# Combined output weights made in other slots, state sums ordered from GpSimd, one partial product in another PSUM bank

## The chip, the cores and the metric

One Trainium2 chip, one core. The metric is the device time of one execution in microseconds, as the median of several runs. The kernel before took 835.33 us (three runs, 834.94 to 835.89). Lines such as L1167 are lines of the kernel before.

## What is computed

Retention attention (scores with a decaying causal mask, no softmax) over 8 batches x 8 heads x 576 positions x 64, then a feed-forward layer with softplus on the 4608 tokens:

```python
scores = (q @ k.T) / 8                                   # per batch and head
Dmat   = where(i >= j, gamma[h] ** (i - j), 0)           # gamma[h] = 1 - 2**(-5-h)
x      = ((scores * Dmat) @ v), heads side by side       # 4608 x 512
h      = x @ w_in                                        # 512 x 2048
g      = maximum(h, 0) + log1p(exp(-abs(h)))
out    = g @ w_out                                       # 2048 x 512
```

All of it is in float32; the large products are made of three products of rounded high and low parts (`TERMS`).

## The kernel before

Tokens go in 9 units of 512. Unit 0 is worked plainly while the weights are split into high and low parts. Units 1 and 2 are worked together, and so are 3 and 4, 5 and 6, 7 and 8: two units make a 2x2 block product that needs seven instead of eight block products (Strassen's form), with sums of input blocks (`T1`, `T2`, `T3`, `NT4`) made beforehand and sums of weight blocks kept in DRAM (`sums_dram` for w_in, `outs_dram`, "outcombined" in the profile, for w_out). Units 1 and 2 use this only for the first product and for the last two of the eight weight pairs J; the last three pairs of units (s = 1, 2, 3) use it for both products.

The parts of the program in order of time:

- about 122 to 195 us: `plain_slot`, twelve slots of unit 1, slot p = 0 to 11
- about 196 to 230 us: `strassen_pair`, J = 6 and J = 7, seven products each
- about 230 to 324 us: twelve plain slots of unit 2, then the outputs of what was kept
- about 324 to 449 us: `full_pair` of s = 1, J = 0 to 7, then `full_phase`, the second product; after that s = 2 (from 506 us) and s = 3.

`product(bank, x)` is six matmuls of 512 columns into one PSUM bank, and the load of a weight block to come. The banks around the change are `acc`, the two halves of `two`, and `later["third"]`. In `full_pair` TensorE does, in this order, the products B11 (into `acc`), B21 (into `y`), T2 (`acc`), T1 (into `z`), T3 (`acc`), B22 (`z`), `second(banks[1])`, NT4 (`acc`), then the attention group (`chunk_products`), then `second(banks[0])`. After B11 ScalarE copies `acc` out (L1167, to a tile of `G[J]`), after T2 again (L1175), after T1 it copies `z` (L1179), after NT4 it copies `acc` (L1208). VectorE adds the others (L1169, L1183, L1197). A product that starts a bank anew must wait until the bank was read.

Every pair with a `group` also carries one attention group of two steps: scores, masked scores times values, the state times queries, and new state sums. `chunk_products` issues them in four stages that put two row groups of the array to work at a time. The state sums of both row groups go into one bank, `third`: the first row group's (t = 0) in stage 1, the second's (t = 1) in stage 4. A tiny copy out of the bank between them (L340, tile `mark`) makes the second wait for the first. After the group VectorE reads the scores (L242), the values (L420) and, after two softplus steps, the state sums (L270, L271, L280).

`full_pair` returns three closures that the next pair runs: `head` after B21, `differences` after T2, and `last_difference` after its `c12` sum (L1246, L1247, then the `jobs` of that pair). ScalarE's logarithms of `c22` (L464, L468, L469) and its copy L1208 come behind these jobs in program order. The program order is the order on each engine (`tc.manual_schedule()`).

The combined output weights are made from `wouts` by `whole_out` (L638, two sums of 512 columns on VectorE), `combine_out` (L648 to L651, four of 256 columns; the last one, L651, still reads the tile that the first cast overwrites), `split_out` (two ScalarE casts L655, two VectorE differences L659) and a store of two 512 KB transfers (L667). There are eight of them, j = 0 to 7. `whole_in(j, at)` puts the sums into the place of the weights 2at and 2at+1; from s = 1 on, `G[at]` is placed there too, so L1167 of pair J = at waits until such a store has read it. Before the change j = 0 and 1 are made in the two `strassen_pair`s, 2, 3 and 4 in slots 4 to 11 of unit 2 (place 0, 1, 2), 5, 6 and 7 among the jobs of `full_pair` at s = 1 (places 4 and 5, and a spare pair of `quad` buffers).

`queue_store` puts the two transfers in the list `queued`; one or more of it is issued at each product, and the rest behind NT4, all on SyncE's queue.

Of the kernel before, what the change touches and what calls it, by code (L numbers as in the profile page):

```python
# [55 lines left out]
RING = 7  # L56
QUADS = 6
B11, B22, B21, T1, T3, T2, NT4 = range(7)
# [25 lines left out]
def retention_softplus_ffn(ctx: ExitStack, tc, first, whole, others, consts, w, out):  # L84
# [50 lines left out]
    place_weights(wpool, WOUT1)  # L135

    live = {}
    states = {}
# [80 lines left out]
    def sums_mm(m, s, t, h):  # L219

        L = live[m]
        start, follows = _chunk_kind(m // 2)
        if follows if t else start != HC:
            nc.tensor.matmul(L["T"][rows[h], t, part[s]], L["kp"][rows[t], s, rows[h]], L["v"][rows[t], s, rows[h]],  # L224
                             start=True, stop=True, skip_group_check=True)

# [83 lines left out]

    def chunk_products(steps, done, marker=nc.vector.tensor_copy):


# [13 lines left out]
        def together(*products):  # L327
            for j in range(2):
                for s in range(2):
                    for o in range(2):  # L330
                        for g, (f, which) in enumerate(products):
                            if j < len(which):
                                t, h = (o, g) if f is scores_mm else (g, o)
                                clear = (j == s == 0,) if f is values_mm else ()
                                f(which[j], s, t, h, *clear)

        together((sums_mm, steps), (scores_mm, steps))
        if steps and _chunk_kind(steps[0] // 2)[0] != HC:
            mark = later["mark"].tile([P, 1], F32, tag="mark", name="mark")
            marker(mark, third[:, 0, 0:1])  # L340
        together((scores_mm, steps), (values_mm, done))
        together((values_mm, done), (cross_mm, done))
        together((cross_mm, done), (sums_mm, steps))


# [601 lines left out]
    def half_b22(i):  # L947
# [10 lines left out]
        (9, finish_combined, 2, nc.vector), (10, prepare_split, 4), (10, prepare_sums, 5), (10, half_b22, 3),  # L958
        (11, prepare_store, 4), (11, finish_combined, 3, nc.vector), (11, prepare_head, 5),
        *[(5 + 2 * j, raw_store, j) for j in range(4)])  # L960
    starts = schedule(*[(3 + 2 * i, start_combined, i) for i in range(CPU)])
# [9 lines left out]
    def strassen_pair(s, J, group, rest, last=False, extra=None):  # L971
# [4 lines left out]
        c = [q[:, n] for q in (quad(), quad()) for n in range(2)]  # L976
        y, z = two[:, 0] if s + 1 < NSUPER else later["third"], two[:, 1]
        product(acc, B11, True)
# [25 lines left out]
        nc.vector.tensor_add(c[2], z, c[2])  # L1004
        if extra is not None:
            combine_rest(raws["out", extra])
        ab2 = logs(c[2])
# [5 lines left out]
        softplus_rest(g, ab)  # L1013
        softplus(c[2], ab2)
        nc.sync.dma_start(kept_dram[J][:, 0], ab2)
        ab3 = logs(c[1])
# [10 lines left out]
        queued_some(len(queued))  # L1027
        if extra is not None:
            combine_store(outs_dram[extra], raws.pop(("out", extra)))
        if group:  # L1030
            chunk_products(*group)
            coming_steps = next_steps(group[0]) if s == 0 and J == NJ - 1 else []
            group_out(*group, between=(finish,))
            for k in coming_steps:
# [22 lines left out]

    extras = {(0, NJ - 2): 0, (0, NJ - 1): 1}
    for s in range(FULL):
# [16 lines left out]
        if first:  # L1076
# [6 lines left out]
                (4, whole_in, 2, 0), (6, combine_out, 2), (7, split_out, 2), (8, store_out, 2),  # L1083
                (8, whole_in, 3, 1), (8, combine_out, 3), (9, split_out, 3), (10, store_out, 3),
                (10, whole_in, 4, 2), (10, combine_out, 4), (11, split_out, 4))
            starts = schedule(*[(min(6 + 2 * i, 2 * first - 1), start_combined, i) for i in range(CPU)])
# [20 lines left out]
        for n, J in enumerate(range(first, NJ)):  # L1107
# [5 lines left out]
            while stores:  # L1113
                prepare_rest(stores[0])
                prepare_store(stores.pop(0))
            if n == 0:
                store_out(4)
            kept_parts(u2, J, kept[n], 1)
# [41 lines left out]
    def full_pair(s, J, group, rest, jobs, more):  # L1160
# [3 lines left out]
        c11, c12, c21, c22 = (g_slot(J, n) for n in range(4))  # L1164
        y, z = two[:, 0], two[:, 1]
        product(acc, B11, True)
# [21 lines left out]
        if not parts_of:  # L1188
            parts_of.extend(moe.tile([P, 2, T], F32R, tag="g", name="parts") for _ in range(2))
            parts_of.extend(later["quad"].tile([P, 2, T], F32R, tag="quad", name="parts") for _ in range(SPLITS - 2))  # L1190
            spare.extend(quad() for _ in range(QUADS - SPLITS + 2))
            banks.extend([ps_y.tile([P, T], F32, tag=f"y{2 * n + m}", name="sum") for m in range(2)] for n in range(2))
# [17 lines left out]
        if group:  # L1210
            chunk_products(*group, nc.scalar.copy)
        ab3 = logs(c12)
# [103 lines left out]
    for s in range(FULL, NSUPER):  # L1316
# [5 lines left out]
        if s == FULL:  # L1322
            for at, f, *args in ((0, whole_in, 5, 4), (0, combine_out, 5), (1, split_out, 5), (1, queue_store, 5),
                                 (2, whole_in, 6, 5), (2, combine_out, 6), (3, split_out, 6), (3, queue_store, 6),
                                 (3, lambda: whole_out(7, spare[:2])), (4, combine_out, 7), (5, split_out, 7),
                                 (5, queue_store, 7)):
                job(at, f, *args)
# [74 lines left out]
```

## Time and profile before

| | |
|---|---|
| median of 3 runs | 835.33 us |
| the profiled execution | 836.63 us, of which the span from the first to the last instruction 834.8 us |
| granted TensorE clock, mean | 0.998 |
| matmul busy | 818.0 us, 98% of the span |
| VectorE, ScalarE, GpSimd busy | 77%, 66%, 20% of the span |
| DMA | 209.93 MB, mean 251 GB/s |

TensorE does matmuls nearly all the time, so the shares of the other engines tell little; what can be read are the places where TensorE sat idle, and what ended each of them. Matmul ends are modelled, so lateness is best read from starts.

### The profile page before, as it was taken

The page shows a single profiled execution, that of the slowest core. Times are in us where ns is not written, and L with a number is a line of the kernel's source. Part 1 is how long each engine was busy: PE and PEld are TensorE (multiplying, and loading weights), DVE is VectorE, ACT ScalarE, POOL GpSimd, SP SyncE. Part 2 cuts the span into 40 slices and gives each one's busy share as a digit, 9 for nine tenths or more (in the row PEclk, how much of TensorE's full clock was granted, in tenths as well). Part 3 has the DMA queues.
Part 4 walks back from the last instruction along what each step waited for, and adds up shares of the span by engine and source line. Part 5 has one row for each costly group of instructions (what it writes and reads, how often), then busy time and mean ns, then how long its engine had stood idle before and what let it go on. Part 6 is the DMA issues. An engine that isn't in the chain of part 4 may idle for free.

```text
span 834.8 us, 19042 instructions
## 1 busy us (share of the span) xinstructions
PE 818.0 (98%) x7322; PEld 666.7 (80%) x7322; DVE 646.6 (77%) x1069; ACT 548.7 (66%) x970; POOL 165.3 (20%) x214
## 2 busy tenths in 40 slices
PE   8999999999999999999999999999999999999998
PEld 6788888887778877877777888888878888888886
DVE  5899975878777897688899995767889955555886
ACT  6778754547744545776777575677785658878653
POOL 3312322440221453112113000211110002212100
PEclk9999999999999999999999999999999999999999
DMA  9888879787789984688888777877856686666675
GB/s 362 305 293 306 303 263 347 256 282 255 243 300 347 322 316 165 216 272 268 265 269 256 215 216 234 263 240 244 254 159 210 207 257 191 194 193 193 193 215 170
DMA packets 149257, 209.93 MB, mean 251 GB/s; under 512 B 10800, under 2 KB 114736, under 8 KB 149168
## 3 DMA queue, kind: packets, MB, share of 16 engines
q1 hardware_dynamic: 149168, 208.72, 75.9%
q8 instruction: 58, 0.95, 0.5%
q14 instruction: 31, 0.25, 0.1%
HBM read 166.74 MB, written 41.94 MB: 250 GB/s over the span
## 4 chain that ended last, share of the span: by engine, by line
PE 69%; DVE 16%; ACT 7%; DMA 4%; issue 3%; POOL 0%; SPq 0%; DVEq 0%; ACTq 0%; POOLq 0%
PE sum L1144 18%; PE acc L839 15%; PE two L839 10%; PE y L491 9%; PE third L839 3%; PE two L1144 3%; PE h L457 2%; PE acc L1144 2%; PE third L1144 2%; PE third L224 2%; ACT parts L1134 1%; DVE g L1154 1%; DVE parts L1138 1%; DVE ab L476 1%; PE two L208 1%
## 5 line engine op out<-in xcount | busy, mean ns | idle before, releaser
L839 PE MATMUL acc<-xt,ring 128*128 128x512 f32 x768 | 193.6, 390 | 1.7 <-DVE quad L1012 0.9
L1144 PE MATMUL sum<-parts,ring 128*128 128x512 f32 x720 | 174.0, 392 | 0.0
L839 PEld LDWEIGHTS acc<-xt,ring 128*128 128x128 f32 x768 | 143.8, 188 | 33.2 <-DVE quad L1012 1.8
L1134 ACT CAST parts<-g 128x512 fp32r<-128x512 f32 x168 | 102.9, 621 | 88.0 <-DVE g L1154 29.9
L1144 PEld LDWEIGHTS sum<-parts,ring 128*128 128x128 f32 x720 | 133.8, 188 | 28.6 <-DVE parts L1138 0.3
L1138 DVE TENSOR_TENSOR parts<-g,parts 128x512 fp32r<-128x512 f32 x168 | 118.5, 727 | 38.0 <-ACT parts L1134 35.7
L491 PE MATMUL y<-wout,g 128*128 128x512 f32 x576 | 140.7, 393 | 0.8 <-DVE g L484 0.8
L491 PEld LDWEIGHTS y<-wout,g 128*128 128x128 f32 x576 | 106.9, 188 | 24.7 <-DVE g L484 1.6
L839 PE MATMUL two<-xt,ring 128*128 128x512 f32 x480 | 122.7, 391 | 0.9 <-DVE quad L981 0.8
L839 PEld LDWEIGHTS two<-xt,ring 128*128 128x128 f32 x480 | 89.5, 188 | 22.0 <-DVE xs L420 1.4
L469 ACT ACTIVATE ab<-ab 128x512 f32<-128x512 f32 x120 | 75.9, 632 | 3.8
L468 ACT ACTIVATE ab<-ab 128x512 f32<-128x512 f32 x120 | 75.9, 633 | 3.5
L1154 DVE SCALAR_TENSOR_TENSOR g<-g,ab 128x512 f32<-128x512 f32 x96 | 67.0, 710 | 7.5 <-ACT ab L469 7.3
L201 POOL TENSOR_TENSOR qv<-qv,consts_sb 128x256 f32<-128x256 f32 x61 | 47.6, 780 | 115.2 <-DMA qv<-others 114.3
L480 ACT CAST g<-ab 128x512 fp32r<-128x512 f32 x44 | 27.3, 621 | 48.2 <-DVE ab L476 36.0
L263 POOL COPY sx<-s 64x256 f32<-64x256 f32 (+1 forms) x34 | 14.1, 414 | 196.3 <-PE third L224 157.7
L457 PE MATMUL h<-xt,win 128*128 128x512 f32 x192 | 47.3, 395 | 1.4 <-DVE x L401 0.7
L282 POOL TENSOR_TENSOR s<-s,consts_sb 128x256 f32<-128x256 f32 (+1 forms) x31 | 20.3, 656 | 135.8 <-DVE s L280 118.3
L464 ACT ACTIVATE ab<-g 128x512 f32<-128x512 f32 x72 | 45.1, 627 | 0.0
L484 DVE TENSOR_TENSOR g<-ab,g 128x512 fp32r<-128x512 f32 x44 | 32.2, 732 | 14.8 <-ACT g L480 14.1
L1241 POOL TENSOR_TENSOR g<-g 128x512 f32<-128x512 f32 x10 | 14.1, 1408 | 149.2 <-DVE g L1154 149.2
L457 PEld LDWEIGHTS h<-xt,win 128*128 128x128 f32 x192 | 35.3, 188 | 9.5 <-DVE win L577 1.4
(190 smaller groups left out, 1356.2 us busy)
## 6 DMA issues: line engine op xcount, KB each, us to landing
ring<-split SPq DMA_DIRECT2D x126, 256.0 KB, 4.6
ring<-combined SPq DMA_DIRECT2D x104, 256.0 KB, 3.5
ring<-outcombined SPq DMA_DIRECT2D x96, 256.0 KB, 3.4
qv<-others SPq DMA_DIRECT2D x61, 320.0 KB, 5.0
ring<-outsplit SPq DMA_DIRECT2D x72, 256.0 KB, 3.6
wst<-w SPq DMA_DIRECT2D x32, 512.0 KB, 5.8
keys<-others SPq DMA_DIRECT2D x61, 256.0 KB, 5.0
split<-win SPq DMA_DIRECT2D x16, 512.0 KB, 6.8
```

The costliest lines, as they stand in the source:

```text
L201: nc.gpsimd.tensor_mul(v, v, f.unsqueeze(2).broadcast_to([P, 4, D]))
L457: nc.tensor.matmul(h, wins[p][:, a, kt * P:(kt + 1) * P], xt[:, b, T1 + kt // 2, kt % 2], start=(n == 0), stop=(n == 3 * NKT - 1))
L464: nc.scalar.activation(ab, h, AF.Abs)
L468: nc.scalar.activation(ab, ab, AF.Exp, scale=-1.0)
L469: nc.scalar.activation(ab, ab, AF.Ln, bias=1.0)
L484: nc.vector.tensor_sub(g[:, LO], ab, g[:, HI].bitcast(F32))
L491: nc.tensor.matmul(ys[u][tt], g[:, a, tt * P:(tt + 1) * P], wouts[p][:, b], start=(p == 0 and n == 0), stop=(p == NF - 1 and n == 2))
L839: nc.tensor.matmul(bank, w[:, ta, kt * P:(kt + 1) * P], xt[:, tb, x, kt], start=start and k == 0, stop=k == 5, skip_group_check=True)
L1134: nc.scalar.copy(t[:, HI], g_slot(J, n))
L1138: nc.vector.tensor_sub(t[:, LO], g_slot(J, n), t[:, HI].bitcast(F32))
L1144: nc.tensor.matmul(bank[m], w[:, a, m * P:(m + 1) * P], t[:, b], start=start and n == 0, stop=n == 2, skip_group_check=True)
L1154: nc.vector.scalar_tensor_tensor(c, c, 0.0, ab, op0=ALU.max, op1=ALU.add)
```

## The change

- `QUADS` goes from 6 to 8 buffers.
- In `full_pair` and `strassen_pair`, `z` (the products T1 and B22) goes to `third` and no longer to the second half of `two`.
- In the attention groups of `full_pair` (`marker` None) the mark is a GpSimd memset of one column, ordered by hand behind the last state sum of the first row group and ahead of the first of the second. All other groups keep the copy on ScalarE or VectorE.
- j = 0 is made in slots 0 to 3 of unit 1. j = 1 stays in `strassen_pair` J = 7, but its two L659 come behind a softplus (L476), and its store behind the attention group and the loads that follow it.
- j = 4 leaves slots 10 and 11 of unit 2 and is made in pair 0 and 1 of s = 1. The work in `last_difference` becomes: pair 0 sums and combination of 4 (place 2); pair 1 split and store of 4, sums and combination of 5 (place 3); pair 2 split and store of 5, sums of 6 (place 4); pair 3 combination, split and store of 6, sums of 7 (place 5); pair 4 combination, split and store of 7. Before it was: pair 1 sums and combination of 5; pair 2 split and store of 5; pair 3 sums and combination of 6; pair 4 split and store of 6, sums of 7; pair 5 combination of 7; pair 6 split and store of 7.

```diff
-QUADS = 6
+QUADS = 8
...
+    ordered = mybir.DependencyInfo(mybir.DependencyClass.Sync, mybir.DependencyReason.DATA)
...
     def chunk_products(steps, done, marker=nc.vector.tensor_copy):
+        halves = [], []
...
-                                f(which[j], s, t, h, *clear)
+                                product_of = f(which[j], s, t, h, *clear)
+                                if product_of is not None:
+                                    halves[t].append(product_of)
 
         together((sums_mm, steps), (scores_mm, steps))
-        if steps and _chunk_kind(steps[0] // 2)[0] != HC:
+        if halves[0] and marker is None:
+            mark = nc.gpsimd.memset(later["mark"].tile([P, 1], F32, tag="mark", name="mark"), 0.0).ins
+            tc.add_manual_dep(mark, halves[0][-1].name, ordered, reason="one bank's first row group")
+        elif steps and _chunk_kind(steps[0] // 2)[0] != HC:
             mark = later["mark"].tile([P, 1], F32, tag="mark", name="mark")
             marker(mark, third[:, 0, 0:1])
         together((scores_mm, steps), (values_mm, done))
         together((values_mm, done), (cross_mm, done))
         together((cross_mm, done), (sums_mm, steps))
+        if halves[0] and halves[1] and marker is None:
+            tc.add_manual_dep(halves[1][0], mark.name, ordered, reason="one bank's second row group")
...
+        (0, whole_out, 0), (1, combine_out, 0), (2, split_out, 0), (3, store_out, 0),
         *[(5 + 2 * j, raw_store, j) for j in range(4)])
...
     def strassen_pair(s, J, group, rest, last=False, extra=None):
-        y, z = two[:, 0] if s + 1 < NSUPER else later["third"], two[:, 1]
+        y, z = two[:, 0], later["third"]
...
         nc.vector.tensor_add(c[2], z, c[2])
-        if extra is not None:
-            combine_rest(raws["out", extra])
         ab2 = logs(c[2])
...
         softplus(c[2], ab2)
+        if extra is not None:
+            combine_rest(raws["out", extra])
...
         queued_some(len(queued))
-        if extra is not None:
-            combine_store(outs_dram[extra], raws.pop(("out", extra)))
         if group:
             chunk_products(*group)
             coming_steps = next_steps(group[0]) if s == 0 and J == NJ - 1 else []
+            if extra is not None:
+                combine_store(outs_dram[extra], raws.pop(("out", extra)))
...
-    extras = {(0, NJ - 2): 0, (0, NJ - 1): 1}
+    extras = {(0, NJ - 1): 1}
...
-                (8, whole_in, 3, 1), (8, combine_out, 3), (9, split_out, 3), (10, store_out, 3),
-                (10, whole_in, 4, 2), (10, combine_out, 4), (11, split_out, 4))
+                (8, whole_in, 3, 1), (8, combine_out, 3), (9, split_out, 3), (10, store_out, 3)                )
...
-            if n == 0:
-                store_out(4)
...
     def full_pair(s, J, group, rest, jobs, more):
-        y, z = two[:, 0], two[:, 1]
+        y, z = two[:, 0], later["third"]
...
         if group:
-            chunk_products(*group, nc.scalar.copy)
+            chunk_products(*group, None)
...
         if s == FULL:
-            for at, f, *args in ((0, whole_in, 5, 4), (0, combine_out, 5), (1, split_out, 5), (1, queue_store, 5),
-                                 (2, whole_in, 6, 5), (2, combine_out, 6), (3, split_out, 6), (3, queue_store, 6),
-                                 (3, lambda: whole_out(7, spare[:2])), (4, combine_out, 7), (5, split_out, 7),
-                                 (5, queue_store, 7)):
+            rest = [lambda: None, lambda: None, lambda: whole_in(4, 2), lambda: combine_out(4)]
+            for at, f, *args in ((0, split_out, 4), (0, queue_store, 4), (0, whole_in, 5, 3), (0, combine_out, 5),
+                                 (1, split_out, 5), (1, queue_store, 5), (1, whole_in, 6, 4), (2, combine_out, 6),
+                                 (2, split_out, 6), (2, queue_store, 6), (2, whole_in, 7, 5), (3, combine_out, 7),
+                                 (3, split_out, 7), (3, queue_store, 7)):
                 job(at, f, *args)
```

(The first number of a job is the pair that returns it; it runs in the next one. The line `spare.extend(...)` still takes four buffers.)

## Rows read from the trace of the kernel before

**Rows 1.** The page, busy time of each engine, its share of the span, and its instructions.

```profile
PE 818.0 (98%) x7322; PEld 666.7 (80%) x7322; DVE 646.6 (77%) x1069; ACT 548.7 (66%) x970; POOL 165.3 (20%) x214
```

**Rows 2.** The waits of TensorE: who waited for whom, us in total, times, longest.

```profile
PE third L224 <- ACT mark L340: 1.5, 3, 0.5
PE third L224 <- POOL qv L201: 1.2, 2, 0.7
```

**Rows 3.** The timeline of TensorE and of ScalarE around the attention group of pair 2 (s = 1): start in us, us, engine, line, operation, tiles, shape, count, and in brackets the idle time before it with what ended it. The first row is the group's first matmul, the third the product after the group.

```profile
368.40 0.27 PE L224 MATMUL third<-qv,keys 64*64 64x64 f32 x1
...
370.67 0.27 PE L224 MATMUL third<-qv,keys 64*64 64x64 f32 x1 [0.54 <-ACT mark L340]
...
371.29 1.66 PE L1144 MATMUL sum<-parts,ring 128*128 128x512 f32 x6
...
370.46 0.16 ACT L340 COPY mark<-third 128x1 f32<-128x1 f32 x1
```

**Rows 4.** GpSimd: a small memset at the start of the program (duration in ns, smallest, median, largest), and its first instruction after the same attention group of pair 2.

```profile
L682 POOL MEMSET mask<- x1: 151/151/151, 1.3 to 1.3; 128x64 f32 x1
...
371.50 0.39 POOL L263 COPY sx<-s 64x256 f32<-64x256 f32 x1 [6.72 <-PE third L224]
```

**Rows 5.** The timeline from the end of pair 3 into pair 4 (s = 1), ScalarE, then TensorE (attention group, `second`, B11, B21, T2), then VectorE.

```profile
382.41 0.63 ACT L464 ACTIVATE ab<-g 128x512 f32<-128x512 f32 x1
...
384.27 0.57 ACT L1208 COPY g<-acc 128x512 f32<-128x512 f32 x1
...
388.84 0.59 ACT L1167 COPY g<-acc 128x512 f32<-128x512 f32 x1 [0.23 <-PE acc L839]
...
383.76 0.27 PE L224 MATMUL third<-qv,keys 64*64 64x64 f32 x1
...
385.78 1.66 PE L1144 MATMUL sum<-parts,ring 128*128 128x512 f32 x6
387.28 1.52 PE L839 MATMUL acc<-xt,ring 128*128 128x512 f32 x6
388.81 1.65 PE L839 MATMUL two<-xt,ring 128*128 128x512 f32 x6
390.30 1.52 PE L839 MATMUL acc<-xt,ring 128*128 128x512 f32 x6
...
384.47 1.28 DVE L638 TENSOR_TENSOR sums<-wout 128x512 f32<-128x512 f32 x2
...
387.14 0.42 DVE L651 TENSOR_TENSOR sums<-sums 128x256 f32<-128x256 f32 x1
...
388.07 0.68 DVE L420 TENSOR_TENSOR xs<-two,consts_sb 128x512 f32<-128x512 f32 x1
```

**Rows 6.** The same place between pair 1 and pair 2: VectorE's last read of the attention group's values, and the product B21 that starts that bank.

```profile
357.92 0.68 DVE L420 TENSOR_TENSOR xs<-two,consts_sb 128x512 f32<-128x512 f32 x1
...
358.65 1.66 PE L839 MATMUL two<-xt,ring 128*128 128x512 f32 x6
```

**Rows 7.** The timeline of `strassen_pair` J = 7, VectorE, then ScalarE, then TensorE (NT4, and the outputs behind the attention group).

```profile
222.16 0.41 DVE L651 TENSOR_TENSOR quad<-quad 128x256 f32<-128x256 f32 x1
...
223.26 1.29 DVE L659 TENSOR_TENSOR quad<-quad 128x512 fp32r<-128x512 f32 x2
...
227.55 0.16 DVE L340 COPY mark<-third 128x1 f32<-128x1 f32 x1
...
222.61 1.14 ACT L655 CAST quad<-quad 128x512 fp32r<-128x512 f32 x2 [3.09 <-DMA ring<-split]
...
225.21 1.66 PE L839 MATMUL acc<-xt,ring 128*128 128x512 f32 x6 [0.88 <-DVE quad L1012]
...
228.82 1.65 PE L491 MATMUL y<-wout,g 128*128 128x512 f32 x6
```

**Rows 8.** Pair 4 into pair 5 (s = 1): the store of j = 6 on SyncE's queue, ScalarE's copy into the place that it reads from, and the product T2 that waits for this copy.

```profile
400.34 0.93 SPq L667 DMA_DIRECT2D outcombined<-sums  x2
...
406.23 0.59 ACT L1167 COPY g<-acc 128x512 f32<-128x512 f32 x1 [1.43 <-PE two L839]
...
406.87 1.43 PE L839 MATMUL acc<-xt,ring 128*128 128x512 f32 x5 [0.70 <-ACT g L1167]
```

**Rows 9.** Behind `strassen_pair` J = 7: the store of j = 1 on SyncE's queue, and GpSimd's scaling of the second step's values for the next attention group.

```profile
229.41 1.03 SPq L667 DMA_DIRECT2D outcombined<-quad  x2
...
239.68 0.61 POOL L201 TENSOR_TENSOR qv<-qv,consts_sb 128x256 f32<-128x256 f32 x1 [0.55 <-DMA qv<-others]
```

**Rows 10.** Slot 11 of unit 2 and what follows: VectorE's split of j = 4, and two waits of TensorE's output products.

```profile
314.85 2.12 DVE L659 TENSOR_TENSOR sums<-sums 128x512 fp32r<-128x512 f32 x2
...
314.99 3.02 PE L491 MATMUL y<-wout,g 128*128 128x512 f32 x12 [0.39 <-DVE g L484]
318.17 1.19 PE L491 MATMUL y<-wout,g 128*128 128x512 f32 x4 [0.17 <-DVE g L484]
```

**Rows 11.** `strassen_pair` J = 6: the products T1 and B22 into `z`, and ScalarE's copy of T1 between them.

```profile
200.31 1.66 PE L839 MATMUL two<-xt,ring 128*128 128x512 f32 x6 [0.84 <-DVE quad L981]
...
203.17 1.07 PE L839 MATMUL two<-xt,ring 128*128 128x512 f32 x4
...
202.16 0.57 ACT L995 COPY quad<-two 128x512 f32<-128x512 f32 x1
```

**Rows 12.** Busy time by stretch, slot 2 of unit 1 with the attention group ahead of it: stretch, length, then TensorE, weight loads, VectorE, ScalarE, GpSimd (instructions), granted clock, DMA share, GB/s.

```profile
132.80:140.20 7.40, 7.40 (x122) 6.08 (x121) 4.65 (x10) 3.16 (x6) 0.61 (x1) 1.00 1.04 360
```

More of the change, by code (lines that the diff above doesn't have):

```diff
@@ L223, in sums_mm @@
         if follows if t else start != HC:
-            nc.tensor.matmul(L["T"][rows[h], t, part[s]], L["kp"][rows[t], s, rows[h]], L["v"][rows[t], s, rows[h]],
-                             start=True, stop=True, skip_group_check=True)
+            return nc.tensor.matmul(L["T"][rows[h], t, part[s]], L["kp"][rows[t], s, rows[h]],
+                                    L["v"][rows[t], s, rows[h]], start=True, stop=True, skip_group_check=True).ins
     def sums(m, bank):
@@ L1190, in full_pair @@
             parts_of.extend(later["quad"].tile([P, 2, T], F32R, tag="quad", name="parts") for _ in range(SPLITS - 2))
-            spare.extend(quad() for _ in range(QUADS - SPLITS + 2))
+            spare.extend(quad() for _ in range(4))
             banks.extend([ps_y.tile([P, T], F32, tag=f"y{2 * n + m}", name="sum") for m in range(2)] for n in range(2))
```

## The prediction

> **What bounds the kernel now.** The page comes first: matmuls are busy for 818.0 of 834.8 us, no other engine over 77% [rows 1]. So the change can only win where TensorE waits or lose by making it wait, and the view to go on with is who TensorE waited for. The change touches these waits: the mark (1.5 us of idle time in three groups), GpSimd's scaling behind late loads (1.2 us) [rows 2], and the single waits of rows 7, 8, 10 and 11. Idle time understates them. The group of pair 2 takes 371.29 - 368.40 = 2.89 us with a late mark [rows 3], that of pair 3 takes 385.78 - 383.76 = 2.02 us without one [rows 5], so a late mark costs 0.87 us, not 0.54. Then the timelines of single engines, read at the places where the change adds work: there one looks for the last thing that a product waits for, and how early it was.
>
> **Slots 0 to 3 of unit 1 (j = 0).** At most the combination (four of 0.42 us, 1.7 us) or the two differences (1.3 us) [rows 7] come into one slot. Slot 2 with its group has 7.40 us, VectorE busy for 4.65 and ScalarE for 3.16 [rows 12]. The idle time of both covers it; taken at 0. If a softplus came late for it, 0 to +1 us. The two further buffers carry no instruction: 0.
>
> **`strassen_pair` J = 6.** T1 waited 0.84 us for the sum that reads the other half of `two` (200.31) [rows 11]; in `third` it needs not. But B22 goes to the same bank and must wait for ScalarE's copy of T1, which ran from 202.16 to 202.73 behind three logarithm steps. B22 can start at 202.8, not 203.17: -0.4 us (bounds -1.0 and 0).
>
> **`strassen_pair` J = 7.** NT4 waited 0.88 us for a sum behind the two L659 (223.26) [rows 7]. They go behind the softplus that ends just before the mark at 227.55, and this mark stays on VectorE: it comes 1.2 to 1.3 us later, at about 228.8. The group would begin 1.0 us earlier, its last stage (0.5 us of 2.0) then starts at 228.95, and the outputs at 229.4 instead of 228.82 [rows 7]. The wait moves from NT4 to the mark: +0.6, or with the 0.4 of J = 6, which moves VectorE's chain too, +0.2. Bounds: -1.4 (the mark not late) and +0.6.
>
> **Loads ahead of the stores.** The two stores took 1.03 us of SyncE's queue ahead of the loads of the next group, whose second step was scaled until 239.68 + 0.61 = 240.29 [rows 9]. Now loads come first, so 1.03 us earlier less the 0.2 above: 239.45. Without its 1.2 us of waiting [rows 2] TensorE would be there at 239.1 + 0.2. Up to this point all of it together gives -0.9 us (bounds -2.4 and +0.3).
>
> **Slots 10 and 11 of unit 2.** The sums, the combination and the split of j = 4 go. Two waits behind VectorE, 0.39 and 0.17 us [rows 10], go with them: -0.6 (bounds -1.0, 0).
>
> **Pairs of s = 1.** Here the removed work comes back, into VectorE's stretch between L1247 and the reads of the group.
>
> Pair 1: before it carried sums and combination, and VectorE's last read of `two` ended at 358.60, B21 of the next pair began at 358.65 [rows 6]. There was no slack left. The split of 4 adds two differences, 0.6 us each back to back (1.29 for two [rows 7]): +1.2 us (bounds 0 and +1.5). The same for pair 0 finds VectorE waiting for TensorE: 0.
>
> Pair 2: the late mark (0.87) goes. But place 3 is now written by the next pair while its store is under way. Pair 4 shows this before the change: store issued at 400.34, L1167 into that place at 406.23, T2 0.70 us late [rows 8], and that although a late mark had given the store 0.87 more. Split and store stand at the same point in pair 2 now. The wait is 0.70 + 0.87 = 1.6; net +0.7 (bounds -0.9, the store landed in time, and +1.2).
>
> Pair 3: combination and split of 6 now stand together. The cast cannot start before the combination's last instruction: in J = 7 the combination ended at 222.57 and the cast began at 222.61, after 3.09 us of idle time [rows 7]. ScalarE does what stands behind only after it. The combination can begin when VectorE is through L1247, at 384.47, and takes 1.7: 386.2; two casts of 0.52 to 0.62: 387.3. The logarithms of `c22` then start at 387.3, not 382.41 [rows 5], 4.9 us late. With them come the copy L1208 (384.27 to 389.2, ended 389.8) and six logarithm steps, so that ScalarE is free for L1167 not at 388.61 (388.84 less its 0.23 of waiting) but at 388.61 + 4.9 - 0.05 (no mark) = 393.45. B11 of pair 4 needs L1208: 389.9 instead of 387.28. T2 needs L1167: 394.1 instead of 390.30 [rows 5]. TensorE is 3.8 us late, less 0.2 for B21's old lateness behind VectorE (388.81): +3.6 (bounds +2.4 and +4.2).
>
> [...]
>
> Pair 4: combination and split of 7, the same. The casts ran at 397.56 in the order before; now they wait for the combination (from about 399.6 to 401.3) and end at 402.4: logarithms 3.8 us later. B11 +1.6, L1167 at 408.4 instead of 406.23 [rows 8], T2 at 409.1 instead of 406.87: +2.2 (bounds +1.0, +3.0). The mark and the store wait that were there are in this difference.
>
> Pairs 5 to 7 lose j = 7's work; pair 6's group lost 0.87 us to the mark, and this goes: -0.9.
>
> **The mark on GpSimd.** It waits for stage 1 of the group, queued ahead of L263 and the state scaling, which nobody needs soon. GpSimd's first instruction after the group of pair 2 started 0.21 us after its end [rows 3, 4], and a memset of 64 columns took 0.15 [rows 4]. Stage 1 is over 0.5 us into the group, stage 4 begins at 1.5: 1.0 us for about 0.5. No wait is left (bounds 0 and +0.5 in each of some 13 groups). For groups where the mark was late by less than a row shows I take -0.5 in all. With the mark still on ScalarE, pairs 3 and 4 would lose more, for it stood behind the held logarithms.
>
> **z in `third`.** In `full_pair` T1 must now wait for the state sums' last read, L280. In VectorE's order this stands ahead of the sum L1169, which the next copy waits for anyway: 0 (bounds -0.3 and +0.3).
>
> **Sum.** -0.9 (to 240 us) - 0.6 + 1.2 + 0.7 + 3.6 + 2.2 - 0.9 - 0.5 = +4.8. The profiled execution took 836.63 us (span 834.8 and 1.8 around it), 1.3 more than the median of 835.33; the difference is put on the median: 840.1 us.
>
> **Rivals.** (1) Slack takes it, faster: the added work in pairs 1 to 4 delays no product, as the mean shares of VectorE and ScalarE (77%, 66%) would suggest [rows 1]. Then 1.2, the 1.6 of pair 2, 3.6 and 2.2 go, pair 4's own mark and store wait (0.87 and 0.70) come off: 4.8 - 8.6 - 1.6 = -5.4, 829.9 us. It decides from one point: L1208 ended at 384.84 and B11 needed it at 387.28 [rows 5], so ScalarE must be less than 2.4 us late; my sum has 4.9. Against it stands the held cast in rows 7. 14%.
> (2) The ScalarE term is half of mine, the rest as summed: combination or casts find VectorE earlier, or the next waits overlap. 4.8 - 2.9 to 4.8 - 5.8: 834.3 to 837.2. 20%, of which 11 stay within the measurement.
> (3) The ordering by hand does not free TensorE, or GpSimd's turn is slower than rows 4 say: the gains at marks (0.87 in pair 2, 0.9, 0.5) are lost, and up to 0.5 us in each of 13 groups is added. 842.4 to 848. 10%.
> Forecast as summed: 56%, 837.5 to 842.5.
>
> **How the numbers follow.** A measurement can tell about 0.2%, 1.7 us. Slower by more: the forecast, rival 3 and the upper part of rival 2 give 56 + 10 + 9 = 75%. Within: 11%. Faster: 14%. The range leaves out about one in ten on each side: below, most of rival 1, above, the end of rival 3: 833.0 to 843.5.
>
> **What would show it.** In the profile after: L655 of pairs 3 and 4 behind 3 to 4 us of ScalarE idle time; B11 of pairs 4 and 5 waiting for L1208, then T2 for L1167; T2 of pair 3 waiting on a copy held by a store; groups of 2.0 us throughout s = 1 and 2; VectorE's mark of J = 7 late; no wait for GpSimd near 240 us. It is wrong if pairs 3 and 4 run in 15 us as before, or if the groups wait for GpSimd.

## The result, and the profile after

The changed kernel took 847.58 us (median of 4 runs) beside 835.52 for the kernel before (4 runs): a ratio of 1.0139, 95% interval 1.0115 to 1.0163. Slower, as forecast, but by 12 us and not by 4.8, and outside the range of 833.0 to 843.5. One of the four, the profiled one, was disturbed (906.69 us at a granted clock of 0.851; the others took 846.10, 846.28 and 848.88, and the ratio is of these), so what follows reads a second profile of the same kernel (run e1 below: 849.55 us, ratio 1.0154, interval 1.0127 to 1.0181; its profiled execution has a span of 847.6).

TensorE is still the bound: 820.9 us of the page's busy time, of 847.6, where [rows 1] have 818.0 of 834.8. So the loss must stand in its waits, 10 of the 12.8 us, with 2.9 of slower work. The page's row of busy times:

```profile
PE 820.9 (97%) x7322; PEld 669.3 (79%) x7322; DVE 643.7 (76%) x1069; ACT 547.4 (65%) x957; POOL 164.1 (19%) x227
```

Who TensorE waited for (us in total, times, longest), which answers to [rows 2]:

```profile
PE acc L848 <- ACT g L1215: 4.5, 2, 2.3
PE acc L848 <- ACT g L1174: 2.8, 3, 1.4
PE third L225 <- issue: 2.0, 1, 2.0
...
PE two L848 <- DVE xs L429: 1.9, 1, 1.9
PE third L225 <- DVE mark L347: 1.5, 1, 1.5
...
PE sum L1151 <- ACT ab L477: 1.4, 1, 1.4
...
PE third L225 <- POOL qv L202: 0.7, 1, 0.7
PE y L500 <- issue: 0.5, 1, 0.5
```

L1215, L1174, L429 and L347 are the forecast ones (L1208, L1167, L420 and L340 before). The two with "issue", where the engine waited for nothing that the profile shows, and the one put down to L477, which that product does not read, are new. To see what each place is worth, take the starts of the 512-column products: there are 3156 in either trace and they come in the same order, so the difference in start of the same product, read at the ends of a stretch, gives what the stretch lost.

| stretch of the kernel before, us | what lies there | forecast | measured (e1) |
|---|---|---|---|
| 0 to 150 | start-up, unchanged | 0 | +1.8 |
| 150 to 166 | slots with j = 0 | 0 | +1.6 |
| 166 to 213 | `strassen_pair` J = 6 | -0.4 | -0.6 |
| 213 to 230 | J = 7 | +0.6 | +0.7 |
| 230 to 248 | loads ahead of stores | -1.1 | -1.5 |
| 248 to 345 | slots 10 and 11 of unit 2 | -0.6 | -1.3 |
| 345 to 361 | pair 1 | +1.2 | +2.0 |
| 361 to 378 | pair 2 | +0.7 | +0.8 |
| 378 to 395 | pair 3 | +3.6 | +3.4 |
| 395 to 412 | pair 4 | +2.2 | +2.3 |
| 412 to 448 | pairs 5 to 7 | -0.9 | -1.4 |
| 448 to 583 | s = 2, pairs 0 to 4 | 0 | +1.0 |
| 583 to 599 | s = 2, pair 5 | 0 | +3.8 |
| 599 to the end | | 0 | 0.0 |

The start-up is spread, not the change: at 150 us the same code stood between -0.5 and +2.0 in the traces of e2 to e12 (+0.1 in e12, +2.0 in e5). The forecast's -0.5 for further marks has no row of its own. What the forecast didn't have is the 1.6 of j = 0 and the 4.8 of s = 2.

Pair 3 into pair 4, which answers to [rows 5]: VectorE's combination of 6, ScalarE's casts of it and what stands behind them, then TensorE's B11 and T2.

```profile
388.15 0.42 DVE L657 TENSOR_TENSOR sums<-sums 128x256 f32<-128x256 f32 x1
...
389.85 1.14 ACT L664 CAST sums<-sums 128x512 fp32r<-128x512 f32 x2 [3.67 <-DVE sums L660]
390.90 0.62 ACT L473 ACTIVATE ab<-g 128x512 f32<-128x512 f32 x1
...
392.76 0.57 ACT L1215 COPY g<-acc 128x512 f32<-128x512 f32 x1
...
393.38 1.64 PE L848 MATMUL acc<-xt,ring 128*128 128x512 f32 x6 [2.30 <-ACT g L1215]
...
397.56 1.67 PE L848 MATMUL acc<-xt,ring 128*128 128x512 f32 x6 [1.18 <-ACT g L1174]
```

The cast starts after 3.67 us of idle time, the logarithms and the copy queue behind it, and TensorE waits twice. This is the forecast's pair 3, step by step. B21 behind pair 1 and T2 behind pair 2, which answer to [rows 6, 8], wait as forecast too; the copy that T2 needs is itself held by a store:

```profile
361.47 1.66 PE L848 MATMUL two<-xt,ring 128*128 128x512 f32 x6 [1.93 <-DVE xs L429]
...
379.00 1.66 PE L848 MATMUL acc<-xt,ring 128*128 128x512 f32 x6 [1.39 <-ACT g L1174]
...
378.36 0.59 ACT L1174 COPY g<-acc 128x512 f32<-128x512 f32 x1 [1.44 <-DMA outcombined<-sums]
```

Pair 4 repeats the first wait of pair 3, and after it TensorE runs at a lower granted clock (0.50, where 1.00 was granted before): six matmuls take 2.47 and 2.34 us, then 1.55 and 1.53. TensorE is so slow here that T2 (416.34) no longer waits for its copy: 1.7 us of clock stand in the place of the forecast's second wait. In e7 below the clock did not fall here, and the second wait came.

```profile
411.89 2.47 PE L848 MATMUL acc<-xt,ring 128*128 128x512 f32 x6 [2.22 <-ACT g L1215]
414.16 2.34 PE L848 MATMUL two<-xt,ring 128*128 128x512 f32 x6
416.34 1.55 PE L848 MATMUL acc<-xt,ring 128*128 128x512 f32 x6
417.73 1.53 PE L848 MATMUL third<-xt,ring 128*128 128x512 f32 x6
```

The same T2 in e7:

```profile
413.50 1.65 PE L848 MATMUL acc<-xt,ring 128*128 128x512 f32 x6 [1.14 <-ACT g L1173]
```

The lower clock in the view by stretch (length, then the engines' busy time and instructions, and the granted clock as the third number from the end): two stretches of 3.4 us at 0.50, the second soon after the wait in pair 5 of s = 2. By estimate each costs half its length, 1.7 us: the three products from 411.89 took 5.84 us, where three at a clock of 1.00 take 4.08 (1.36 each in the chain of work near 594).

```profile
412.50:415.90 3.40, 3.40 (x10) 2.62 (x9) 1.87 (x4) 3.31 (x6) 0.10 (x1) 0.50 1.03 312
601.90:603.60 1.70, 1.64 (x15) 1.35 (x15) 1.24 (x3) 0.47 (x1) 0.39 (x1) 1.00 0.16 60
603.60:607.00 3.40, 3.40 (x10) 2.62 (x9) 2.43 (x6) 0.38 (x1) 0.61 (x1) 0.50 0.40 137
```

J = 7, which answers to [rows 7]: the two L668 stand ahead of the mark on VectorE, as forecast. The last row is the mark on GpSimd in pair 3: it ends 0.6 us ahead of its group's fourth stage (388.84), and no group of s = 1 or 2 waited for it.

```profile
230.91 0.69 DVE L668 TENSOR_TENSOR quad<-quad 128x512 fp32r<-128x512 f32 x1
231.52 0.15 DVE L347 COPY mark<-third 128x1 f32<-128x1 f32 x1
...
388.16 0.10 POOL L343 MEMSET mark<- 128x1 f32 x1 [4.38 <-PE third L225]
```

### The profile page after: what moved, and what is told of

Read it like the earlier page. It is cut to its first block, busy times and chain, and to the rows that moved or that the text cites. A ratio compares the mean times of both kernels' runs of the same rounds, so it can differ in the third digit from the quotient of the medians.

```text
span 905.0 us, 19070 instructions
## 1 busy us (share of the span) xinstructions
PE 890.1 (98%) x7322; PEld 683.7 (76%) x7322; DVE 645.7 (71%) x1069; ACT 551.5 (61%) x957; POOL 163.9 (18%) x227
## 4 chain that ended last, share of the span: by engine, by line
PE 90%; DVE 5%; ACT 3%; DMA 1%; issue 1%; SPq 0%; DVEq 0%
PE acc L848 19%; PE sum L1151 19%; PE y L500 16%; PE third L848 11%; PE h L466 5%; PE two L848 4%; PE two L1151 3%; PE acc L1151 2%; PE third L1151 2%; PE third L225 2%; PE two L209 1%; PE two L287 1%; PE two L299 1%; DVE parts L1145 1%; DMA raw<-whole 1%
## 5 line engine op out<-in xcount | busy, mean ns | idle before, releaser
L848 PE MATMUL acc<-xt,ring 128*128 128x512 f32 x768 | 212.4, 417 | 4.0 <-ACT g L1215 2.1
L1151 PE MATMUL sum<-parts,ring 128*128 128x512 f32 x720 | 190.3, 418 | 1.5 <-ACT ab L478 1.5
L848 PEld LDWEIGHTS acc<-xt,ring 128*128 128x128 f32 x768 | 146.9, 192 | 50.9 <-ACT g L1215 3.1
L1151 PEld LDWEIGHTS sum<-parts,ring 128*128 128x128 f32 x720 | 137.0, 192 | 42.7 <-DVE xs L429 1.4
L500 PE MATMUL y<-wout,g 128*128 128x512 f32 x576 | 153.6, 419 | 0.0
L500 PEld LDWEIGHTS y<-wout,g 128*128 128x128 f32 x576 | 109.6, 192 | 33.3 <-issue 0.4
L848 PE MATMUL third<-xt,ring 128*128 128x512 f32 x444 | 122.0, 417 | 0.0
L848 PEld LDWEIGHTS third<-xt,ring 128*128 128x128 f32 x444 | 85.2, 192 | 26.2
L477 ACT ACTIVATE ab<-ab 128x512 f32<-128x512 f32 x120 | 75.9, 632 | 3.5
L466 PE MATMUL h<-xt,win 128*128 128x512 f32 x192 | 51.5, 421 | 0.9 <-DVE x L410 0.6
L848 PE MATMUL two<-xt,ring 128*128 128x512 f32 x168 | 46.6, 417 | 0.2 <-DVE xs L429 0.2
## 6 DMA issues: line engine op xcount, KB each, us to landing
ring<-split SPq DMA_DIRECT2D x126, 256.0 KB, 4.1
ring<-combined SPq DMA_DIRECT2D x104, 256.0 KB, 3.4
ring<-outcombined SPq DMA_DIRECT2D x96, 256.0 KB, 3.3
ring<-outsplit SPq DMA_DIRECT2D x72, 256.0 KB, 3.6
keys<-others SPq DMA_DIRECT2D x61, 256.0 KB, 4.5
```

Of the source, the lines that this page charges most:

```text
L466: nc.tensor.matmul(h, wins[p][:, a, kt * P:(kt + 1) * P], xt[:, b, T1 + kt // 2, kt % 2], start=(n == 0), stop=(n == 3 * NKT - 1))
L477: nc.scalar.activation(ab, ab, AF.Exp, scale=-1.0)
L500: nc.tensor.matmul(ys[u][tt], g[:, a, tt * P:(tt + 1) * P], wouts[p][:, b], start=(p == 0 and n == 0), stop=(p == NF - 1 and n == 2))
L848: nc.tensor.matmul(bank, w[:, ta, kt * P:(kt + 1) * P], xt[:, tb, x, kt], start=start and k == 0, stop=k == 5, skip_group_check=True)
L1151: nc.tensor.matmul(bank[m], w[:, a, m * P:(m + 1) * P], t[:, b], start=start and n == 0, stop=n == 2, skip_group_check=True)
```

## The experiments

Theory 1 is the forecast's own: in s = 1 the split held behind the combination makes ScalarE, and with it TensorE, late. Against it stood theory 2, that the loss lies elsewhere: in e1 a lower clock or a longer start or end, in e2 and e3 the other parts of the change. Theory 3 was formed after the first four runs. Below, "at 166 us" means the difference in start to the kernel before, as in the table.

**e1: the kernel after, unchanged.**

> The changed kernel once more, for a profile at the same granted clock as that of the kernel before. Theory 1 (the pairs of s = 1 are late by held casts, late VectorE and stores): at a clock of 0.998 the span is some 9.6 us over the kernel before (844.4 against 834.8); of this pairs 1 to 5 of s = 1 hold 6 to 8 us, with B11 of pairs 4 and 5 each 1.5 to 2.7 us late behind L1215 and T2 about 1.5 us late behind L1174. Theory 2 (a lower granted clock, or a start or an end that became longer): the pairs hold under 3 us, and the excess is spread evenly or lies outside of 324 to 450 us.

849.55 us. Its profile is the one above: 8.5 us from 345 to 412, as theory 1 has it or a little more, and 4.8 in s = 2, which neither theory named.

**e2: the jobs back in the pairs of the kernel before** (and j = 4 in slots 10 and 11 of unit 2).

```diff
-            rest = [..., lambda: whole_in(4, 2), lambda: combine_out(4)]
-            for at, f, *args in ((0, split_out, 4), (0, queue_store, 4), (0, whole_in, 5, 3), (0, combine_out, 5),
+            for at, f, *args in ((0, whole_in, 5, 4), (0, combine_out, 5), (1, split_out, 5), (1, queue_store, 5),
...
```

> The changed kernel with j = 4 back in slots 10 and 11 of unit 2 and the jobs of full_pair as before; marks on GpSimd, z in third, j = 0 in unit 1, loads ahead of stores stay. Theory 1: all that the change lost is in these jobs, so the rest of it is a gain: 828 to 833 us, faster than the kernel before by 3 to 7 us. Theory 2: still 840 us or more, because the loss is not in the jobs.

840.80 us, ratio 1.0055 (1.0028 to 1.0081). The jobs are worth what theory 1 says: s = 1 (345 to 448 us) now gains 1.7 where e1 loses 7.2. But its 828 to 833 did not come, and the kernel isn't faster than before, for s = 2 loses 7.7 (3.4 of it in two stretches at the lower clock). A part of the loss has nothing to do with the jobs.

**e3: the kernel before with the jobs alone** (and their buffers).

> The kernel before with only the jobs of full_pair as in the change and j = 4 among them (mark on ScalarE, z in two, six buffers, j = 0 in J = 6). Theory 1: slower than the changed kernel, 848 to 856 us, for in pairs 3 and 4 the mark on ScalarE stands behind the held logarithms and the attention group waits some 3.5 us in each. Theory 2: within 2 us of the kernel before.

847.92 us, ratio 1.0139 (1.0110 to 1.0167). From 345 to 412 us it loses 14.8, and nothing in s = 2. So the loss of s = 2 belongs to the other parts. Of the 14.8 some 6 are the clock: stretches of 3.4, 6.8 and 3.4 us at the lower clock (at 361.2, 391.9 and 415.8), in which TensorE sat idle for 1.6 us; half of the rest is lost, by the same estimate.

**e4: the combinations of 6 and 7 one pair earlier than their splits.**

```diff
-  (1, whole_in, 6, 4), (2, combine_out, 6), (2, split_out, 6), (2, queue_store, 6), (2, whole_in, 7, 5), (3, combine_out, 7),
+  (1, whole_in, 6, 4), (1, combine_out, 6), (2, split_out, 6), (2, queue_store, 6), (2, whole_in, 7, 5), (2, combine_out, 7),
```

> The changed kernel with the combinations of 6 and 7 one pair earlier (behind the sums, in pairs 2 and 3), so that a cast never stands right behind its combination; the same instructions otherwise. Theory 1: the waits behind L1215 go, 3 to 5 us less than the changed kernel (841 to 843.5 us at the same clock); what is left is VectorE's lateness in pairs 1 to 3 and the waits on stores. Theory 1b (VectorE's load in these pairs is the bound, not the hold): less than 1.5 us off, because the same work then holds the reads of the group in pairs 2 and 3.

841.57 us, ratio 1.0073 (1.0046 to 1.0100). s = 1 loses 2.1 and not 7.2, so the held cast is worth 5.0, where the forecast has 5.8 for pairs 3 and 4. Of the 5.0 the clock is 1.7: it did not fall in e4. And the 5.0 are net, since the moved work now makes VectorE late for B21 of pairs 2 to 4 (4.8 us in three waits, 1.9 in one in e1).

**What the waits of s = 2 have in common.** In e1, e2 and e4 they stand at the same instructions of TensorE, counted from the program's start: number 10687 (pair 0) and 12480 (pair 5), and in e1 and e4 a third, in unit 1, at 3519: each 191 or 192 above a multiple of 256. Such an instruction is called a boundary below; the boundary ahead of 12480 is 12224. Queue q8 of the page's DMA list moves 58 packets of 16 KB in the span, one for about 260 of TensorE's 15,067 instructions. In the trace of the kernel before, TensorE begins 13,826 instructions between the start of the fourth packet and that of the last: 256.0 for each of these 54 packets. One such packet starts just ahead of each wait. For pair 5 of e1, the DMA view's row of q8 in the 0.1 us from 599.50 (packets, MB, and the packet's time as a share of 16 engines in 0.1 us, which is 0.95 us):

```profile
q8 instruction: 1, 0.02, 59.2%
```

and the chain of work that ended last there (start, us, what):

```profile
599.95 2.01 issue
601.96 0.21 PE third L225
```

The packet is there at 600.50, and the next product begins at 601.96. In the sixteen such waits of over 0.4 us in unit 1 and s = 2 of all traces, the product begins 1.18 to 1.55 us after the packet's end. That is theory 3: TensorE's own instructions come late. No row says so in words; it rests on the place and on these times.

**e5 and e6: instructions moved against the boundaries.** 16 products of 64 x 64 into a free bank ahead of pair 0 of s = 2 in the kernel after (e5), 5 in the kernel before (e6).

```diff
+        if s == FULL + 1 and J == 0:
+            L = live[group[0][0]]
+            for _ in range(16):
+                nc.tensor.matmul(later["third"][rows[0], 0:D], L["kp"][rows[0], 0, rows[0]], L["v"][rows[0], 0, rows[0]], ...)
```

> The kernel after, with 16 extra products of 64 x 64 into a free bank ahead of pair 0 of s = 2, whose results nobody reads; nothing else is moved. Theory 3 (TensorE's own instructions come late): in the kernel after, the two waits in s = 2 that no engine explains (1.5 and 2.2 us) stand at TensorE's instructions number 10687 and 12480, both 191 or 192 above a multiple of 256, each beside a 16 KB transfer of the instruction queue. The 16 products with their loads of weights move all later instructions by some 32 to 64 against these marks, so the waits should go, and with them the two stretches of half clock: 3 to 5 us less than the kernel after, about 843.5 to 846.5. Rival (the mark on GpSimd or z in the third bank makes them): both waits stay at the same products, and the time is that of the kernel after plus 0.5.

> The kernel before, with 5 such products of 64 x 64 ahead of pair 0 of s = 2, so that its groups stand to the multiples of 256 instructions about as those of the kernel after do. No mark on GpSimd and no z in the third bank here. Theory 3: waits of 1.5 to 2.3 us that no engine explains appear in the groups of s = 2, in pair 0 or pair 5 or both, 2 to 5 us more than the kernel before (838 to 841). Rival: nothing appears, 0.2 us more.

e5: 845.24 us, ratio 1.0109 (1.0081 to 1.0136), 4.3 under e1; both waits are gone, though the 16 products themselves took 2.1 us. e6: 836.30, ratio 1.0011 (0.9993 to 1.0029), and no wait appears, though the boundaries stand as in the kernel after to within some 12 instructions (one of its ten executions took 841.50; it was not profiled, and its cause isn't known). The place in the count is needed but isn't enough: theory 3 as it stood is half refuted. The traces show what is missing. In e1 the packet for pair 5 starts 3.71 us after TensorE begins boundary 12224; in e6 it starts 0.04 us ahead of that. In e6 TensorE's semaphore instruction for this group is done at 585.64, 2.8 us ahead of the group's first product; in e1 it lasts from 595.22 to 596.29, and the group begins at 597.98. One of the two semaphores that it waits for is raised by VectorE's instructions alone, and it ends 0.05 us after this one:

```profile
595.56 0.68 DVE L1204 TENSOR_TENSOR g<-third,g 128x512 f32<-128x512 f32 x1
```

This is VectorE's sum of B22, which now reads z in `third`, the bank that the group's state sums write. In pair 0 of e1 a semaphore instruction on VectorE stands there too (523.71, 0.05 us after that pair's sum); e9 below, without z in `third`, has none there. Not shown is what lies between the end of TensorE's wait ahead of pair 5 in e1 (596.29) and the packet's start, 3.3 us later.

**e7: j = 0 back in J = 6.** The line with slots 0 to 3 goes, `extras` is as before.

> The kernel after, with the weights of j = 0 made in J = 6 of the first Strassen pair again and not in slots 0 to 3 of unit 1. The products at 166 us of the kernel after stand 1.6 us later against the kernel before than those at 150 us. If j = 0 costs this (a late scaling by GpSimd of 0.81 and a wait of 0.70), it goes: at 166 us no more than at 150, and, with J = 6 carrying the work again (+0 to +1.0), 847 to 849. If it is only the spread of the start, nothing is gained: 849.5. By theory 3 the waits in s = 2 stay if the count of TensorE's instructions there is the same within a few.

845.20 us, ratio 1.0096 (1.0067 to 1.0125). +0.9 at 150 and +0.9 at 166 us: the 1.6 is gone, and J = 6 shows the same gain of 0.6 with the work as without. The time is below the 847 to 849 expected; in the profiled execution the lower clock behind pair 4 and behind pair 5 of s = 2 did not come, and pair 4 lost 1.7 by its two waits alone.

**e8: the marks of s = 1 and 2 on ScalarE again** (`chunk_products(*group, nc.scalar.copy)`).

> The kernel after, with the marks in s = 1 and 2 on ScalarE again. As the prediction has it, pairs 3 and 4 of s = 1 then lose more, since the mark stands behind the held logarithms (up to 3.5 us each), and late marks return elsewhere (0.87 in pairs 2 and 6): 4 to 9 us more than the kernel after in s = 1. Rival (the mark on GpSimd is itself the cost in s = 2): the two waits of 1.5 and 2.2 us in s = 2 go, and the time falls by 3 to 5 there. Theory 3: they go only if the instructions' count moves.

850.06 us, ratio 1.0161 (1.0135 to 1.0187). s = 1 loses 11.5, 4.3 more than e1. The groups of pairs 3 and 4 wait 4.3 and 4.1 us for the mark (8.9 in three groups), in the place of the waits behind L1215, and two stretches of 6.8 us at the lower clock (0.50) overlap and follow. An estimate of the clock's part: in the 13.6 us TensorE was busy for 10.3, half of which is lost, 5.2 against 1.7 in e1; so 3.5 of the 4.3 are the clock. s = 2 loses 0.5: without the marks' semaphores the count of TensorE's instructions there is 11 lower, and the instructions behind the boundary begin just late enough (1.5 us after the packet in pair 0; pair 5 waits 0.4). As a test of the mark in s = 2 it is inconclusive for this reason.

**e9 and e10: z in `third` taken out of s = 2 of the kernel after (e9); put into e6 (e10).**

```diff
-        y, z = two[:, 0], later["third"]
+        y, z = two[:, 0], later["third"] if s == FULL else two[:, 1]     # e9
-        y, z = two[:, 0], two[:, 1]
+        y, z = two[:, 0], later["third"]                                  # e10
```

> The kernel after, with z in the third bank in s = 1 only; in s = 2 it is the second half of two again. [...] With z in third the first state sum of a group waits for VectorE's sum of B22 as well; in the kernel after this held the sequencer for 1.07 us ahead of pair 5 of s = 2 (595.22 to 596.29), and the request of the next instructions behind it. Without that wait the transfer of pair 5 starts earlier, so the wait of 2.2 us there goes and that of pair 0 shrinks or goes: 2.5 to 4.5 us less than the kernel after (845 to 847). Rival (the mark on GpSimd in s = 2 is enough): both waits stay, 849.5.

> The kernel before with the 5 extra products ahead of s = 2 (which alone changed nothing) and z of the full pairs in the third bank; marks on ScalarE, jobs as before. Theory 3: both conditions are there, a multiple of 256 at the start of a group and a sequencer held by the wait for VectorE, so one or both waits of 1.5 to 2.3 us appear in pair 0 and pair 5 of s = 2, 2 to 5 us in s = 2 against the kernel before. Rival (GpSimd's mark makes the waits): s = 2 takes as long as in the kernel before.

e9: 841.76 us, ratio 1.0069 (1.0049 to 1.0088). s = 2 (448 us to the end) loses 0.1, where e1 loses 4.7; the packets start 0.61 us ahead of the boundary before (pair 0) and 0.68 behind it (pair 5). e10: 840.82, ratio 1.0050 (1.0033 to 1.0066): the wait of pair 5 appears at instruction 12480, in the kernel before, with marks on ScalarE, and here too TensorE's semaphore instruction lasts for 1.07 us, until VectorE's sum is done (588.73 to 589.79). Pair 0 shows no wait. Who TensorE waited for most in e10, and its chain at that place:

```profile
PE two L298 <- issue: 2.3, 1, 2.3
```

```profile
593.14 2.33 issue
595.47 0.27 PE two L298
```

With e6 and e5 that is all four cases of pair 5: the place alone (e6, e9) does nothing, the wait for VectorE's sum alone (e5) does nothing, and with both together (e1, e2, e4, e7, e10, e12) the product behind the group comes 2.0 to 2.6 us later; in e1, e2, e10 and e12 1.7 us at the lower clock follow. The GpSimd mark isn't needed for it.

**e12: the two stores of j = 0 one slot later.** `(3, store_out, 0)` becomes `(4, store_out, 0)`.

> The kernel after, with the two stores of j = 0 issued one slot later (slot 4 of unit 1 in place of 3), and nothing else moved. In the kernel after they took 2.12 us of SyncE's queue at 152.20, ahead of the loads for the next attention group, whose scaling by GpSimd then came 0.81 us late; a wait of 0.70 followed on TensorE's own instructions. If the place in SyncE's queue is the whole cost of j = 0, the products at 166 us stand against the kernel before as those at 150 us do (+1.6 in the kernel after, now within 0.2), and the time is 1.5 less than after's 849.55, about 848, within the spread of runs. Rival (VectorE's sums and split in slots 0 to 2 delay something): 1.0 or more of the 1.6 stays.

847.87 us. The products stand at +0.06 at 150 and at 166 us: the place of the stores in SyncE's queue is the whole 1.6. SyncE's issues of e1, and GpSimd's scaling behind them:

```profile
152.20 2.12 SPq L676 DMA_DIRECT2D outcombined<-quad  x2
154.43 1.93 SPq L618 DMA_DIRECT2D ring<-split  x2
...
158.09 0.38 SPq L167 DMA_DIRECT2D qv<-others  x1
...
163.64 0.80 POOL L202 TENSOR_TENSOR qv<-qv,consts_sb 128x256 f32<-128x256 f32 x1 [1.09 <-DMA ring<-split]
```

and of e12, where the load leaves 4.6 us earlier and the scaling is done at 160.81, 0.8 us ahead of the group's first product (161.64); in e1 that product stood at 163.38, and the scaling ended at 164.44:

```profile
153.48 0.38 SPq L167 DMA_DIRECT2D qv<-others  x1
153.91 1.20 SPq L676 DMA_DIRECT2D outcombined<-quad  x2
...
159.91 0.90 POOL L202 TENSOR_TENSOR qv<-qv,consts_sb 128x256 f32<-128x256 f32 x1 [0.91 <-DMA qv<-others]
```

**e11: the parts that gained.** The jobs as in e2, j = 0 as in e7, z as in e9, and the mark of J = 7 on GpSimd too (`chunk_products(*group, None)` in `strassen_pair`).

> The parts of the change that gained, without those that lost: marks on GpSimd in the full pairs and in J = 7, loads ahead of stores, z in third in the Strassen pairs and in s = 1 but not in s = 2; the weights of all j made in the places of the kernel before. By the traces so far: to 345 us -0.8 without j = 0's 1.1 in unit 1, -1.0 to -1.3 for the mark of J = 7, in s = 1 -1.7, in s = 2 nothing if theory 3 holds (the waits of 1.5 and 2.2 us and the half clock behind them gone): 830 to 832. If the waits of s = 2 stay, 834 to 836. If GpSimd is late in J = 7 with its scalings, 831 to 833.

831.86 us, ratio 0.9952 (0.9938 to 0.9965): 4.1 us faster than the kernel before. At 230 us it has gained 1.0 (the mark of J = 7 is nobody's wait any more), at 248 us 2.5, and s = 1 adds 1.5. TensorE's longest wait on another engine's work behind the start is 1.0 us. The page's busy times, and its two largest waits there:

```profile
PE 816.7 (98%) x7322; PEld 665.6 (80%) x7322; DVE 648.0 (78%) x1068; ACT 546.8 (66%) x957; POOL 165.4 (20%) x228
```

```profile
PE two L848 <- DVE xs L429: 1.5, 3, 0.8
PE two L1153 <- DVE parts L1147: 1.3, 2, 1.0
```

## Why the prediction was wrong

Its main mechanism was right, and so was the size of most terms; two terms taken as 0 were not 0.

- **Pairs of s = 1**: +6.8 forecast, +7.2 measured, each pair within 0.8. The held cast (behind 3.67 us of idle time in e1, against 3.09 in [rows 7]; the logarithm after it, whose input VectorE's L1190 had written by 384.93, began at 390.90), then L1208 and L1167, came as worked out in pair 3; e4 shows that it is the hold, and e2 that the jobs carry all of the loss in s = 1. Pair 1 was 0.8 too small, outside its bounds: B21 waited 1.93 for VectorE. That pair 4 came out at +2.3 for +2.2 is in part luck: in e1 1.7 of it is the lower clock, of which the forecast has nothing, in the place of T2's wait for L1167; e7, with both waits and no lower clock, has +1.7. And the gain in pairs 5 to 7 is that of the work of j = 7, not of the mark: with marks on ScalarE (e3, e8) it is the same -1.4.
- **J = 6, J = 7, loads, slots 10 and 11**: -1.5 forecast, -2.7 measured; every sign was right, the gains at the loads and in slots 10 and 11 were larger (the latter, -1.3, outside the bounds of -1.0 and 0).
- **Mark on GpSimd**: "No wait is left" held. Of the -0.5 taken for further groups one shows: 0.4 in pair 0 of s = 2, where e5, e9 and e11 gain it and e3 and e8 don't. That pairs 3 and 4 would lose more with the mark on ScalarE held too (e8, e3), but most of it through the clock.
- **Slots 0 to 3 of unit 1**: "The idle time of both covers it; taken at 0" failed, +1.6. Cover was looked for on VectorE and ScalarE. The step also moves two stores, and in SyncE's queue these stand ahead of the next group's loads: the very thing for which the prediction credited the loads after J = 7 (e12). Two steps from one product to the next make it up, too long by 0.9 (the wait for GpSimd) and 0.7 us (at instruction 3519, where the 16 KB packet starts 2.7 us after the group's first product, in e12 1.1). That the first wait makes this packet late is likely, but not shown.
- **z in `third`**: "0 (bounds -0.3 and +0.3)" failed, +4.7 (e9 against e1). The step asked what T1 would wait for, and not what the next writer of `third`, the group's first state sum, would. That wait costs nothing by itself, since VectorE is done before the group begins (596.24 and 597.98 in e1). With it a semaphore instruction of TensorE lasts for 1.07 us (e1, e10), and the packet of instructions comes late (3.71 us after boundary 12224 begins in e1, 0.68 in e9); that the two together with the place in the count make the loss is shown by e5, e6, e9 and e10, how the first brings the second is not. Of the 4.7 the lower clock is 1.7. No row of the kernel before could give this price, but the new wait could be seen in the order of reads and writes.

With these two the sum is 840.1 + 1.6 + 4.7 = 846.4. What is left to 847.58 and 849.55 is in the spread of the runs and the start-up of e1. The rivals fell: slack took nothing (1), the term wasn't half (2), and GpSimd wasn't slow (3), though the time lay in (3)'s interval for another reason (by its own terms that interval ends at 848.9, not 848).

Open: what sets the start of an instruction packet (in the kernel before the one behind boundary 12480 starts 8 us after it, at 600.74 for 592.52, without z in `third`), why the product follows the packet's end by 1.2 to 1.5 us, what z in `third` costs at the instruction count of the kernel before (no run has that alone), and after which waits the lower clock comes in which execution (e2, at the same program, ran between 837.2 and 843.8).

## What to carry to other kernels

Of a step that is moved, list every queue that it enters: here two stores of 2.12 us on SyncE cost more than all the arithmetic that came with them. When a bank changes its user, ask what its next writer must now wait for as well, also where the data is early. With dense groups of small matmuls such as these, keep semaphore waits that can be late out of the few us ahead of the group, as e9 does (s = 2 loses 0.1 there and 4.7 in e1), or shift the group against the instruction count, as e5 does (4.3 us under e1).

## What the runs showed that was not expected

TensorE's instruction stream was the limit in pair 5 of s = 2, as far as place and times tell: a group of about 256 instructions in 2.0 us waited when the packet of the next 16 KB started 1.4 to 1.6 us behind the group's first product (e10, e1), and not when it started 0.8 to 1.0 us ahead of it (e6, e9). The packet took 0.9 to 1.4 us, and another 1.2 to 1.5 passed until the next product. The pair lost 2.0 to 2.6 us by it; the profile calls the wait "issue" or names an engine that had long been done. The kernel after has 27 semaphore instructions more in its 15,067, and where the boundaries fall in a group hangs on such counts.
